# First transfers in order on one queue, the flag through a transfer within SBUF, and spare matmuls in pieces of 176 columns

## The chip, the cores and the metric

One core of a Trainium2 chip. The metric is device time in microseconds of one execution; a median of several executions is given with its range. A profile is one of these executions, and its span is 1.5 to 1.9 us shorter than the device time.

## The reference

```python
# x, f_logit: (4, 6080, 256) fp32; lower_bound: (256,); w_in: (256, 2048), w_out: (2048, 256) float64
f = lower_bound + (1 - lower_bound) * sigmoid(f_logit)
for t in range(S):                          # gated recurrence along the sequence
    h = f[:, t] * h + (1 - f[:, t]) * x[:, t]
    y[:, t] = h
z = y.reshape(24320, 256) @ w_in
out = (z - tanh(z)) @ w_out
```

## The kernel before

The kernel works on blocks of 512 tokens (the first has 256). Weights are 64-bit in memory and are rounded to fp32 on DVE and ACT; block 0 and block 1 are transposed on PE; the recurrence is a scan on DVE; the rest is fp32 matmuls in a Strassen scheme. z - tanh(z) is a polynomial that holds for small z only, so a flag is computed, and at the end every engine reads it and branches over a general version of the kernel. The parts that the change touches:

```python
def fetch_half(u, s, raw, queues):          # first weights: two halves of 256 KB on two queues
    ...
    for i, queue in enumerate(queues):
        part = slice(i * n, (i + 1) * n)
        queue.dma_start(out=dst[:, part], in_=src[s, u][:, part])

def keep_busy(n):                           # spare matmuls on zeros, "K1.n" in the order below
    for _ in range(2 * n):
        nc.tensor.matmul(busy[:, 0:HB], lhsT=zeros..., rhs=zeros...[:, 0:HB], ...)   # HB = 256

def sum_up():                               # the flag: sum over partitions by a matmul
    most = ps_b.tile([P, 2, HB], FP32, name="most", tag="D")
    nc.tensor.matmul(most[0:1, 0, 0:1], lhsT=worst[:], rhs=ones[:], start=True, stop=True)
    nc.scalar.copy(out=flag[:], in_=most[0:1, 0, 0:1])

open_by(["W.0"])                            # first weights, halves on SP and ACT
nc.gpsimd.dma_start(out=lb[:], in_=lower_bound...)
load(0, 0, nc.scalar)                       # f_logit of block 0 on ACT's queue; all else on SP

before = """
    K1.8 ce.0 cr.0 dx.0 cm.0 cx.0 tf.0 cs.0 W.1 tx.0 cb.0 sg0.0 L K1.8 sg1.0 cw.0
    df.1 f0.0 v0.0 f1.0 ce.1 cr.1 v1.0 dx.1 cm.1 cx.1 tf.1 sc0.0 cs.1 W.2 tx.1
    sg0.1 cb.1 sg1.1 sc1.0 K1.1 cw.1 f1.1 F.0.0.0 v1.1 f0.1 W.3 v0.1 cr.2 F.0.0.1
    sc1.1 t.0.0.0 sc0.1 q.0.0.0 K1.3 t.0.0.1 cm.2 F.1.0.0 ...
"""  # issue order: K1 spare, ce..cw weight rounding, tf/tx transposes, sc scans, F matmuls
```

So PE's order is: 16 spare matmuls, transposes of f_logit and x of block 0, 16 spare ones (the second group), transposes of f_logit and x of block 1, 2 spare ones, the first real matmuls (block 0), 6 spare ones (the third group), real matmuls of block 1, and then real work to the end.

Of the kernel before, what the change touches and what calls it, by code (L numbers as in the profile page):

```python
# [9 lines left out]
FP32 = mybir.dt.float32  # L10
# [5 lines left out]
BF16 = mybir.dt.bfloat16  # L16
PSUM = bass.MemoryType.PSUM
P = 128
# [13 lines left out]
def kernel(  # L32
# [25 lines left out]
    nc = tc.nc  # L58

    B, S, D = x.shape  # L60
    DFF = moe_w_in.shape[1]
    N = B * S
    KC = D // P
    TB = 512
    HB = TB // 2
# [18 lines left out]
    const = ctx.enter_context(tc.tile_pool(name="const", bufs=1))  # L84
# [4 lines left out]
    worst = const.tile([P, 1], FP32, name="worst")  # L89
    ones = const.tile([P, 1], FP32, name="ones")  # L90
    flag = const.tile([1, 1], FP32, name="flag")
    zeros = const.tile([P, TB], FP32, name="zeros")
    ident = const.tile([P, P], FP32, name="ident")

# [6 lines left out]
        for s in range(2):  # L101
            queue.dma_start(out=dst[:, :, s], in_=src[s, u])

    def fetch_half(u, s, raw, queues):

        src = moe_w_in.rearrange("(p k) (s u f) -> s u p k f", k=KC, s=2, u=NU)
        dst = raw.rearrange("p (k f) -> p k f", k=KC)
        n = KC // len(queues)
        for i, queue in enumerate(queues):
            part = slice(i * n, (i + 1) * n)  # L110
            queue.dma_start(out=dst[:, part], in_=src[s, u][:, part])

    def fetch_w_out(u, raw, queue):

# [139 lines left out]
    def fast(ctx):  # L254
# [19 lines left out]
        ps_b = ctx.enter_context(tc.tile_pool(name="ps_b", bufs=1, space=PSUM))  # L274
# [9 lines left out]
        order = [(0, 0, 0), (0, 0, 1), (0, 1), (1, 0), (0, 2), (1, 1), (0, 3), (1, 2), (1, 3)]  # L284

        def fetch_weight(i):
            kind, u = order[i][0:2]
            if len(order[i]) == 3:
                raw = Tpool.tile([P, TB], INT64, name="raw", tag="Tg")
                queues = (nc.sync, nc.scalar) if i == 0 else (nc.sync,)  # L290
                fetch_half(u, order[i][2], raw[:], queues)
            else:
                raw = rawpool.tile([P, KC * TB], INT64, name="raw")
                (fetch_w_in, fetch_w_out)[kind](u, raw[:], nc.sync)
            raws[i] = raw
# [256 lines left out]
        def end(j):  # L552


            hb, n = sizes[j] // 2, j * NU + NU - 1
            C = acc[j, "C"][:, 0 : 4 * hb].rearrange("p (n t) -> p n t", n=4)
            osb = opool.tile([P, NQ, D], FP32, name="osb", tag="osb")
            alone = [ps_a.tile([P, TB], FP32, name="A", tag="A")[:, 0:hb] for _ in range(2)]
            for half, (slot, right, q) in enumerate(((A22, "T", 2), (S4, "h", 2))):
                for c in range(2):  # L560
                    nc.tensor.matmul(
                        alone[half],
                        lhsT=w_out[NU - 1][:, slot, c * P : (c + 1) * P],
                        rhs=piece(n, right)[:, q, c],
                        start=c == 0,
                        stop=c == 1,
                    )
            for half in range(2):
                slot = 2 - half
                nc.vector.tensor_tensor(  # L570
                    out=C[:, slot], in0=alone[half], in1=C[:, slot], op=ALU.add
                )
            for half in range(2):
                for i in range(2):
                    name = ("Qa", "Qb", "Qc", "D")[2 * half + i]
                    bank = ps_b.tile([P, KC, P], FP32, name=name, tag=name)
                    for k in (0, 1) if half == 0 else (1, 0):
                        nc.tensor.transpose(
                            bank[:, k], C[:, 2 * k + half, i * P : (i + 1) * P], ident[:]
                        )  # L580
                    (nc.scalar.copy, nc.vector.tensor_copy)[i](
                        out=osb[:, 2 * half + i].rearrange("p (m k) -> p k m", k=KC),
                        in_=bank[:],
                    )
                t0 = starts[j] + half * hb
                nc.sync.dma_start(
                    out=out[t0 : t0 + hb, :].rearrange("(i p) d -> p i d", p=P),
                    in_=osb[:, 2 * half : 2 * half + 2],
                )
# [29 lines left out]
            o3=lambda j: finish(j, 3),  # L619
# [26 lines left out]
        for word in around.split():  # L646
            name, u, at = re.fullmatch(r"([a-zA-Z0-9]+)(?:\.(\d))?([+-]\d)?", word).groups()
# [5 lines left out]
                return natpool.tile([P, NQ, D], FP32, name=name, tag=name)  # L653
            return opool.tile([P, NQ, D], FP32, name=name, tag="osb")

        def load(j, s, queue=nc.sync):

            nat = spot(j, ("fn", "xn")[s])
            queue.dma_start(
                out=nat[:, 0 : sizes[j] // P],  # L660
                in_=srcs[s][starts[j] : starts[j] + sizes[j], :].rearrange(
                    "(n p) d -> p n d", p=P
                ),
            )
            nats[j, s] = nat
# [138 lines left out]
        def p_give(j):  # L804
# [15 lines left out]
            W=fetch_weight,  # L820
            df=lambda j: load(j, 0) if j < TURNED else fetch(j, (0,)),
# [60 lines left out]

        def sum_up():

            most = ps_b.tile([P, 2, HB], FP32, name="most", tag="D")
            nc.tensor.matmul(
                most[0:1, 0, 0:1], lhsT=worst[:], rhs=ones[:], start=True, stop=True
            )
            nc.scalar.copy(out=flag[:], in_=most[0:1, 0, 0:1])

        def turn_and_fetch(j):
            steps["tx"](j)
# [2 lines left out]

        def keep_busy(n):

            for _ in range(2 * n):
                nc.tensor.matmul(  # L899
                    busy[:, 0:HB], lhsT=zeros.bitcast(BF16)[:, 0:P],  # L900
                    rhs=zeros.bitcast(BF16)[:, 0:HB], start=True, stop=True,
                    skip_group_check=True,
                )

# [17 lines left out]
        def open_by(words):  # L922
            for word in words:
                name, *at = word.split(".")
                at = [int(i) for i in at]
                if name in opening:
                    opening[name](*at)
                else:
                    steps[name](at[0] * NU + at[1] if len(at) == 2 else at[0])

        with tc.manual_schedule():
            nc.vector.memset(zeros[:], 0.0)
            nc.vector.memset(ones[:], 1.0)

            open_by(["W.0"])
            nc.gpsimd.dma_start(
                out=lb[:], in_=lower_bound.rearrange("(p k) -> p k", k=KC)
            )
            load(0, 0, nc.scalar)
            make_identity(nc, ident[:])  # L940

            nc.scalar.activation(out=flag[:], in_=ones[0:1, :], func=AF.Sigmoid)
            busy = ps_b.tile([P, TB], FP32, name="B", tag="B")
            open_by(before.split())
            for cycle in range(PLAIN + 1, NBLK + 3):
                for name, u, at in turns:
                    j = cycle + at
                    if not PLAIN <= j < NBLK:
                        continue
                    final = j == NBLK - 1  # L950
                    if final and (name, u) == ("Qd", NU - 1):
                        continue
                    if u is None:
                        if final and name == "o1":
                            nc.vector.reduce_max(
                                out=worst[:], in_=flags[:], axis=mybir.AxisListType.X
                            )
                        if final and name == "o3":
                            sum_up()
                        if final and name == "o4":  # L960
                            end(j)
                        if final and name[0] == "o":
                            if name in ("o1", "o2", "o3"):
                                part_end(j, name)
                            continue
                        steps[name](j)
                        if name == "tx" and j + 1 < NBLK:
                            fetch(j + 1)
                        if final and name == "p15":
                            part_end(j, name)  # L970
                        continue
                    steps[name](j * NU + u)
                    if final and (name, u) == ("Qd", NU - 2):
                        kept = mixpool.tile([P, 4, HB], FP32, name="T")
                        acc[j, "kept"] = kept
                        nc.scalar.copy(
                            out=kept[:, 0:2], in_=acc[j, 3][:, :, 0 : sizes[j] // 2]
                        )
# [172 lines left out]
```

## Time and profile before

| | before |
|---|---|
| time, median of 3 runs | 2329.25 us (2329.11 to 2329.95) |
| span of the profile | 2328.2 us |
| PE busy | 2319.0 us |
| landing of f_logit of block 0 / x of block 1 | 6.73 / 11.50 us |
| last copy ends / last store lands | 2322.78 / 2327.03 us |

PE busy is the whole span (2319.0 of 2328.2 us), so only what moves PE's first real work or what follows its last work can count. The times in the last two rows are from the timeline and from the records of landings. The lines are in the prediction.

The trace's record of a granted clock of 1.00 begins at 10.04 us here. Spare matmuls of 256 columns last 421 ns and start 213 ns apart before it, and last 272 ns and start 109 to 110 apart after it: the prediction and the expectations call this cold or half clock, and warm. In the records of landings f_logit's semaphore rises 16 times, 15 of them by 6.21 us and the last at 6.73, and PE's transposes of it start at 6.86; so the last of the 16 is what I call the landing.

### The profile page before, as it was taken

The numbers are of one execution on the slowest core, as the hardware profiler recorded it, in microseconds if no ns is written. First come the engines' busy times: TensorE is split into PE (matmuls) and PEld (weight loads), VectorE is DVE, ScalarE is ACT, GpSimd is POOL, SyncE is SP. The second block draws the span as 40 slices with busy tenths as digits, with TensorE's granted clock in tenths as the row PEclk, the third lists the DMA queues.
The fourth block names the chain that finished last, engine by engine and source line by source line (L and its number), as shares of the span: only waits on it lengthen the run. The fifth ranks groups of instructions, "written<-read, shape, count | busy, mean of one in ns | idle before, by whom it ended". The sixth has DMA issues, their size and how long they took to land.

```text
span 2328.2 us, 28719 instructions
## 1 busy us (share of the span) xinstructions
PE 2319.0 (100%) x10699; PEld 2027.8 (87%) x10699; DVE 2122.3 (91%) x2451; ACT 1801.8 (77%) x2688; POOL 1.4 (0%) x7
## 2 busy tenths in 40 slices
PE   9999999999999999999999999999999999999998
PEld 6888888888888888888888888888888888888887
DVE  9999899998999989999999999999899998999988
ACT  7777777777777777777777777777777777777775
POOL 0000000000000000000000000000000000000000
PEclk9999999999999999999999999999999999999999
DMA  5301111111111111112111121111211112111101
GB/s 170 70 19 34 39 37 28 28 37 37 37 28 28 39 34 37 28 28 41 32 37 28 28 45 28 37 28 28 46 28 36 28 28 46 31 34 28 28 10 28
DMA packets 296831, 85.00 MB, mean 37 GB/s; under 512 B 289776, under 2 KB 292592, under 8 KB 296688
## 3 DMA queue, kind: packets, MB, share of 16 engines
q1 hardware_dynamic: 296240, 82.61, 16.5%
q8 instruction: 84, 1.38, 0.2%
q14 instruction: 59, 0.48, 0.1%
q10 hardware_dynamic: 416, 0.52, 0.1%
q0 software_dynamic: 32, 0.00, 0.0%
HBM read 58.20 MB, written 24.90 MB: 36 GB/s over the span
## 4 chain that ended last, share of the span: by engine, by line
PE 99%; DMA 0%; DVE 0%; ACTq 0%; issue 0%
PE A L392 27%; PE Qa L475 14%; PE Qb L475 14%; PE D L392 14%; PE Qd L475 14%; PE Qc L475 7%; PE B L392 7%; PE Qa L795 1%; PE Qb L795 1%; PE Qc L795 1%; PE A L728 1%; PE D L728 0%; PE Qd L728 0%; DMA fn<-in_f_logit_dram 0%; PE B L728 0%; PE B L899 0%
## 5 line engine op out<-in xcount | busy, mean ns | idle before, releaser
L392 PE MATMUL A<-T,w_in 128*128 128x256 f32 x2208 | 558.8, 379 | 0.0
L392 PEld LDWEIGHTS A<-T,w_in 128*128 128x128 f32 x2208 | 419.5, 190 | 57.0
L436 DVE TENSOR_TENSOR h<-h,q 128x1024 f32<-128x1024 f32 x368 | 437.4, 1219 | 3.2
L430 DVE SCALAR_TENSOR_TENSOR q<-q,t 128x1024 f32<-128x1024 f32 x368 | 439.8, 1215 | 0.0
L423 ACT ACTIVATE q<-t 128x1024 f32<-128x1024 f32 x368 | 382.7, 1053 | 46.2 <-DVE h L436 43.3
L420 ACT ACTIVATE t<-h 128x1024 f32<-128x1024 f32 x368 | 388.6, 1056 | 3.1 <-DVE h L407 0.3
L441 ACT ACTIVATE junk<-t 128x1024 bf16<-128x1024 f32 x368 | 388.2, 1055 | 1.5
L455 DVE TENSOR_TENSOR Tg<-h 128x1024 f32<-128x1024 f32 x368 | 348.0, 946 | 6.4
L475 PE MATMUL Qb<-h,w_out 128*128 128x256 f32 x1472 | 347.7, 379 | 0.0
L475 PEld LDWEIGHTS Qb<-h,w_out 128*128 128x128 f32 x1472 | 279.7, 190 | 38.0
L475 PE MATMUL Qa<-Tg,w_out 128*128 128x256 f32 x736 | 218.9, 379 | 0.0
L475 PE MATMUL Qa<-h,w_out 128*128 128x256 f32 x736 | 218.9, 379 | 0.0
L404 ACT COPY h<-B 128x512 f32<-128x512 f32 x184 | 107.0, 581 | 144.3 <-PE B L392 95.6
L475 PE MATMUL Qd<-Tg,w_out 128*128 128x256 f32 x732 | 217.7, 379 | 0.0
L475 PE MATMUL Qd<-h,w_out 128*128 128x256 f32 x732 | 217.7, 379 | 0.0
L404 ACT COPY h<-A 128x512 f32<-128x512 f32 x184 | 107.0, 581 | 139.4 <-PE A L392 128.0
L407 DVE TENSOR_TENSOR h<-D,r 128x512 f32<-128x512 f32 x184 | 126.8, 689 | 90.3 <-PE D L392 89.2
L407 DVE TENSOR_TENSOR h<-A,r 128x512 f32<-128x512 f32 x184 | 126.2, 686 | 76.6 <-PE A L392 43.6
L392 PE MATMUL D<-y,w_in 128*128 128x256 f32 x736 | 188.9, 379 | 0.0
L392 PE MATMUL B<-y,w_in 128*128 128x256 f32 x736 | 188.9, 379 | 0.0
L392 PE MATMUL A<-y,w_in 128*128 128x256 f32 x736 | 188.9, 379 | 0.0
L392 PE MATMUL D<-T,w_in 128*128 128x256 f32 x736 | 188.9, 379 | 0.0
(137 smaller groups left out, 2996.6 us busy)
## 6 DMA issues: line engine op xcount, KB each, us to landing
fn<-in_f_logit_dram SPq DMA_DIRECT2D x184, 128.0 KB, 3.1
xn<-in_x_dram SPq DMA_DIRECT2D x184, 128.0 KB, 3.2
out_dram<-osb SPq DMA_DIRECT2D x180, 128.0 KB, 2.8
raw<-in_moe_w_out_dram SPq DMA_DIRECT2D x8, 512.0 KB, 4.5
raw<-in_moe_w_in_dram SPq DMA_DIRECT2D x7, 512.0 KB, 6.6
out_dram<-osb SPq DMA_DIRECT2D x3, 256.0 KB, 4.2
fn<-in_f_logit_dram SPq DMA_DIRECT2D x1, 512.0 KB, 7.4
xn<-in_x_dram SPq DMA_DIRECT2D x1, 512.0 KB, 8.2
```

Source lines behind the costliest of these rows:

```text
L392: nc.tensor.matmul(ps[:, c], lhsT=w_in[u][:, slot, c * P : (c + 1) * P], rhs=mixes[j][right], start=start and c == 0, stop=True, skip_grou ...
L404: nc.scalar.copy(out=dst, in_=piece(n, bank))
L407: nc.vector.tensor_tensor(out=piece(n, "h")[:, q], in0=piece(n, bank), in1=piece(n, r), op=ALU.add)
L420: nc.scalar.activation(out=half(n, i, "t"), in_=half(n, i), func=AF.Square)
L423: nc.scalar.activation(out=half(n, i, "q"), in_=half(n, i, "t"), func=AF.Square, scale=RA, bias=RB,)
L430: nc.vector.scalar_tensor_tensor(out=q, in0=q, scalar=RC, in1=t, op0=ALU.add, op1=ALU.mult)
L436: nc.vector.tensor_tensor(out=h, in0=h, in1=q, op=ALU.mult)
L441: nc.scalar.activation(out=junk[:, :, :, 0 : st[n]["hb"]], in_=t, func=AF.Relu, bias=-TINY, accum_out=flags[:, 2 * n + i : 2 * n + i + 1],)
L455: nc.vector.tensor_tensor(out=o, in0=a, in1=b, op=ALU.subtract)
L475: nc.tensor.matmul(acc[j, part][:, r, 0 : st[n]["hb"]], lhsT=w_out[u][:, slot, c * P : (c + 1) * P], rhs=piece(n, right)[:, q, c], start=( ...
L728: nc.tensor.matmul(h[c], lhsT=w_in[u][:, 2 * k + s, c * P : (c + 1) * P], rhs=ys[j][:, k, 0:nb], start=k == 0 and (c == 0 or len(banks) == 2),
L795: nc.tensor.matmul(acc[j][i // 2][:, i % 2].rearrange("p (k m) -> p k m", k=2), lhsT=plain[j, u][:, s, c, i * P : (i + 1) * P], rhs=w_out[ ...
```

## The change

The intent: let f_logit land sooner by not sharing the queues, take lower_bound off GpSimd's queue (5.5 us from issue to landing there), take the flag's matmul off PE, and cut the spare matmuls finer.

```diff
-            queues = (nc.sync, nc.scalar) if i == 0 else (nc.sync,)
-            fetch_half(u, order[i][2], raw[:], queues)
+            fetch_half(u, order[i][2], raw[:], nc.sync)
...
             for half in range(2):          # end(): the last two additions on DVE
                 ...
+            look()
...
         def sum_up():
-            most = ps_b.tile([P, 2, HB], FP32, name="most", tag="D")
-            nc.tensor.matmul(most[0:1, 0, 0:1], lhsT=worst[:], rhs=ones[:], ...)
-            nc.scalar.copy(out=flag[:], in_=most[0:1, 0, 0:1])
+            nc.sync.dma_start(out=row[:], in_=worst[:])
+        def look():
+            nc.vector.reduce_max(out=flag[:], in_=row[:], axis=mybir.AxisListType.X)
...
-                        if final and name == "o3":     # now right after `worst` is made
                             sum_up()
...
-            for _ in range(2 * n):
-                nc.tensor.matmul(busy[:, 0:HB], ... rhs=zeros...[:, 0:HB], ...)
+            for _ in range(3 * n):
+                nc.tensor.matmul(busy[:, 0:176], ... rhs=zeros...[:, 0:176], ...)
...
-            open_by(["W.0"])
-            nc.gpsimd.dma_start(out=lb[:], in_=lower_bound...)
-            load(0, 0, nc.scalar)
+            nc.scalar.dma_start(out=lb[:], in_=lower_bound...)
+            open_by(["W.0", "df.0"])
```

I call the three parts **queues** (transfers), **flag** and **columns** (spare matmuls).

More of the change, by code (lines that the diff above doesn't have):

```diff
@@ L91 @@
     flag = const.tile([1, 1], FP32, name="flag")
+    row = const.tile([1, P], FP32, name="row")
     zeros = const.tile([P, TB], FP32, name="zeros")
@@ L102, in fetch_w_in, with fetch_half @@
             queue.dma_start(out=dst[:, :, s], in_=src[s, u])
-    def fetch_half(u, s, raw, queues):
+    def fetch_half(u, s, raw, queue):
         src = moe_w_in.rearrange("(p k) (s u f) -> s u p k f", k=KC, s=2, u=NU)
-        dst = raw.rearrange("p (k f) -> p k f", k=KC)
-        n = KC // len(queues)
-        for i, queue in enumerate(queues):
-            part = slice(i * n, (i + 1) * n)
-            queue.dma_start(out=dst[:, part], in_=src[s, u][:, part])
+        queue.dma_start(out=raw.rearrange("p (k f) -> p k f", k=KC), in_=src[s, u])
     def fetch_w_out(u, raw, queue):
@@ L654, in spot, with load @@
             return opool.tile([P, NQ, D], FP32, name=name, tag="osb")
-        def load(j, s, queue=nc.sync):
+        def load(j, s):
             nat = spot(j, ("fn", "xn")[s])
-            queue.dma_start(
+            nc.sync.dma_start(
                 out=nat[:, 0 : sizes[j] // P],
@@ L883, in sum_up @@
         def sum_up():
-            most = ps_b.tile([P, 2, HB], FP32, name="most", tag="D")
-            nc.tensor.matmul(
-                most[0:1, 0, 0:1], lhsT=worst[:], rhs=ones[:], start=True, stop=True
-            )
-            nc.scalar.copy(out=flag[:], in_=most[0:1, 0, 0:1])
+            nc.sync.dma_start(out=row[:], in_=worst[:])
+        def look():
+            nc.vector.reduce_max(out=flag[:], in_=row[:], axis=mybir.AxisListType.X)
         def turn_and_fetch(j):
@@ L896, in keep_busy @@
         def keep_busy(n):
-            for _ in range(2 * n):
+            for _ in range(3 * n):
                 nc.tensor.matmul(
-                    busy[:, 0:HB], lhsT=zeros.bitcast(BF16)[:, 0:P],
-                    rhs=zeros.bitcast(BF16)[:, 0:HB], start=True, stop=True,
+                    busy[:, 0:176], lhsT=zeros.bitcast(BF16)[:, 0:P],
+                    rhs=zeros.bitcast(BF16)[:, 0:176], start=True, stop=True,
                     skip_group_check=True,
@@ L933, in fast @@
             nc.vector.memset(ones[:], 1.0)
-            open_by(["W.0"])
-            nc.gpsimd.dma_start(
+            nc.scalar.dma_start(
                 out=lb[:], in_=lower_bound.rearrange("(p k) -> p k", k=KC)
             )
-            load(0, 0, nc.scalar)
+            open_by(["W.0", "df.0"])
             make_identity(nc, ident[:])
```

## The prediction

> **What bounds the kernel now.** I read the page's summary first, then the waits of the PE alone, then the chain and the timeline of the two ends of the span.
>
> ```profile
> PE 2319.0 (100%) x10699; PEld 2027.8 (87%) x10699; DVE 2122.3 (91%) x2451; ACT 1801.8 (77%) x2688; POOL 1.4 (0%) x7
> ...
> PE 99%; DMA 0%; DVE 0%; ACTq 0%; issue 0%
> ...
> PE B L899 <- DVE ones L933: 1.7, 1, 1.7
> PE Qa L673 <- DMA fn<-in_f_logit_dram: 1.6, 1, 1.6
> ```
>
> The PE is busy for the whole span, the chain that ends last is 99% PE, and the list of PE waits has two entries in the whole run: 1.7 us until the first spare matmul may start, and 1.6 us for the first f_logit block. After that it never stands still until the last stores. So only the first 17 us (before the last gap that is filled with spare matmuls) and the last 10 us can change; the 2300 us between are untouched by the diff. The head, from the chain:
>
> ```profile
> 1.43 5.30 DMA fn<-in_f_logit_dram
> 6.73 0.14 issue
> 6.86 0.67 PE Qa L673 x2
> ...
> 8.82 2.41 PE B L899 x16
> 11.23 0.48 PE Qa L673 x4
> ...
> 13.36 3.46 PE A L728 x16
> 16.82 0.66 PE B L899 x6
> 17.47 1.72 PE Qa L728 x4
> ```
>
> f_logit lands at 6.73 us and from there to 17.47 us the PE is the chain: transposes of block 0, 16 spare matmuls, transposes of block 1, the first real matmuls at 13.36, six spare ones, the next real ones at 17.47. DVE runs nearly full beside it, from the landing of the first weights:
>
> ```profile
> 5.50 0.43 DVE L142 TENSOR_SCALAR e<-raw 128x512 int32<-128x512 int32 x1 [3.85 <-DMA raw<-in_moe_w_in_dram]
> 8.51 0.48 DVE L694 SCALAR_TENSOR_TENSOR v<-fT,om,Qc 128x256 f32<-128x256 f32 x1
> 11.76 0.68 DVE L235 TENSOR_TENSOR_SCAN y<-f,v 128x256 f32<-128x256 f32 x1
> 13.25 0.75 DVE L694 SCALAR_TENSOR_TENSOR v<-fT,om,Qd 128x512 f32<-128x512 f32 x1 [0.23 <-PE Qd L673]
> 14.57 2.45 DVE L235 TENSOR_TENSOR_SCAN y<-f,y,v 128x512 f32<-128x512 f32 x2
> ```
>
> The scan that the first real matmuls need ends at 11.76+0.68 = 12.44, and the one that the matmuls at 17.47 need ends at 14.57+2.45 = 17.02. So the spare matmuls hide little: DVE is at most 0.9 us and then 0.45 us ahead of the PE. That caps what an earlier f_logit can give. The tail, from the timeline:
>
> ```profile
> 2319.14 0.19 PE L886 MATMUL most<-ones,worst 128*1 128x1 f32 x2
> 2321.29 0.42 DVE L570 TENSOR_TENSOR C<-A,C 128x256 f32<-128x256 f32 x1 [0.16 <-PE A L561]
> 2321.77 0.42 DVE L581 COPY osb<-Qb 128x256 f32<-128x256 f32 x1
> 2322.26 0.97 SPq L586 DMA_DIRECT2D out_dram<-osb  x2
> 2322.36 0.42 DVE L581 COPY osb<-D 128x256 f32<-128x256 f32 x1 [0.16 <-PE D L578]
> ```
>
> The flag's matmul sits on PE's path to the end; the last copy ends at 2322.78, and the second of the last stores lands 4.2 us after its issue at about 2322.84, so at 2327.0 of a span of 2328.2.
>
> [...](1) [...]SP and ACT packets alternate from 2.5 us on, and the total is 350 to 390 GB/s with one queue (7 to 14 us) as with two. (2) [...]15 of f_logit's 16 marks are written by 6.24 us, the last at 6.71. (3) [...]The trace records a granted clock of 1.00 only from 10.52 us on, and spare matmuls last 421 ns at first and 272 later. (4) [...]the trace has (3.60-0.42)/15 = 212 ns in the first group and 0.66/6 = 110 ns in the last[...].
>
> **The change part by part.**
>
> *One queue for first weights, f_logit, x.* Before, the two halves of the weights (256 KB each) ran on two queues at once and f_logit queued behind one half while x queued behind the other, so f_logit's packets took turns with x's and with the second weights. In order on one queue the laggard engine writes 16 weight packets of 2 KB, then 16 packets of 1 KB for f_logit (about 45 ns each by the packet records, 0.72 us), then 16 for x. The weights' last mark was at 5.34 us and may come 0.1 us earlier, since no packet of x gets in between; I take 5.2 to 5.3. f_logit's is then 5.25+0.72 = 6.0 instead of 6.71: 0.7 us earlier. x's is 6.7 instead of 6.25, but PE needs it only after four f_logit transposes (0.86 us), so it costs nothing. What follows (second weights, block 1) has the same bytes ahead of it as before and lands as before: the transposes of x of block 1 were due at 3.25+8.2 = 11.45.
>
> *lower_bound on ACT's queue.* It moves 1 KB ahead of everything in place of 7.0 us (issue 1.48 plus 5.5). Its reader ran at 7.85 behind a sigmoid that waited for PE, so it ended no wait. It may put 0.1 us of tiny packets in front of the weights.
>
> *Spare matmuls.* 40 of 256 columns become 60 of 176: 3x176 = 528 columns for 512, 3% more. The first group ends, cold, at 1.71+24x0.147 = 5.2 plus drain, still ahead of f_logit. The second: 24x0.147 = 3.5 us if cold throughout, 24x0.076 = 1.8 if warm (estimates from place 4). Before it took 2.41 with the clock change inside it. The gap in PE's work shrinks from 1.6 to 0.8 us[...]. So: block 0 transposes from 6.1, with x done by 7.9; second group until 9.7 (warm) to 11.0 (cold until 10.5); block 1's last transposes then end by 12.45 (bound by x at 11.45 plus 8 of 0.12) to 12.9; three spare ones 0.23; first real matmuls at 12.7 to 13.1 instead of 13.36.
>
> Next the cap: DVE gains about 0.2 at the start (it waited from cw at 8.39 until Qc for 0.12, and the weights land 0.1 sooner), and its wait of 0.23 for block 1's x shrinks, so its scan ends 0.2 to 0.5 before 17.02. PE's step at 17.47 then comes at about 12.7+3.46+0.68 = 16.85 to 17.2. The head gives **0.3 to 0.65 us, I take 0.55**.
>
> *Flag by a transfer within SBUF.* It removes two matmuls from the PE path (0.12 us in the chain, up to 0.15 with the wait before). It adds a transfer of 128 elements of 4 bytes behind four output stores on SP, issued at about 2319.1; those stores' last marks are at 2321.40, so the row can land at about 2321.6 to 2321.75. The reduce in DVE's stream waits for that, where the last addition now ends at about 2321.6. The reduce takes about 0.25 us (estimate: DVE's copy of 256 columns takes 0.42, half the columns and the same fixed part). So the copy of Qb starts at about 2322.0 for 2321.77; the copy of D, bound by PE until now at 2322.36, stays there; SP's second store is issued about 0.1 later. **Tail: +0.1.** There is one more effect: the flag is known at 2322.0 instead of 2319.5. GpSimd read it at 2319.5 and its instruction fetches ran at 2320.2 and 2322.1, clear of the last stores. Now all engines branch together, and instruction packets meet the stores: in the trace one engine's marks came at 2326.36 and 2327.08, where the other 15 were done at 2325.44, beside an instruction packet of 16 KB that lasted 0.93 us. I add 0.1 for it, with much doubt. Sum: -0.55+0.1+0.1 = about -0.4, so 2329.25-0.4 = **2328.8 us**.
>
> **The rivals.** (a) *DVE becomes the bound in the head*: the weights land no sooner, or later because one queue generates 512 KB in 0.66 us instead of two doing 256 KB in 0.41, and lower_bound's packets precede them. For it: DVE's full timeline from 5.50 to 17 us. Against it: packets started at 2.51, long after both issues. It would leave a gain of 0.1 to 0.2 and a time of 2329.2. (b) *The flag's row lands late*, at 2322.3 or more, and both copies and stores wait: +0.5 to +0.8, time 2329.4 to 2329.7. For it: it queues behind 512 KB of packets of 256 bytes. Against it: those are done by 2321.4. (c) *The laggard engine of the last stores goes free*, because the branches come at another time: up to 2327.08-2325.44 = 1.6 us less, time about 2327.6. (d) *f_logit was hidden anyway* by the spare matmuls: no change in the head, 2329.4. Against it: the recorded 1.6 us wait.
>
> **Range and chances.** The head can give 0 to 0.7, the tail -1.5 to +0.8, and the three runs before spread over 0.84 us: 2327.8 to 2329.8. Two per cent is 46 us, and no end of this kernel has that: 0.99 for within.
>
> **What would show it.** Right: f_logit lands near 6.0, x near 6.7, first real matmuls near 12.8 and the ones after the six (now nine) spare at about 16.9; DVE's wait at 13.25 gone; the reduce ends near 2322.0, D's copy near where it was less the head's gain. Wrong: weights landing after 5.5, a new PE wait on a scan, or a DVE wait of over 0.5 us for the row. A change between 20 and 2310 us would contradict the whole argument.

## The result, and the profile after

| | before | after |
|---|---|---|
| time, median of 6 runs each | 2329.18 us (2328.82 to 2329.95) | 2329.20 us (2329.06 to 2329.84) |
| span of the profile | 2328.2 us | 2327.4 us |

The ratio is 1.0, 95% interval 0.9987 to 1.0013. (The ratio is not quite the ratio of the medians.) The times are the same; the 0.8 us between the two profiles is not a gain, since the profiled run of before (2329.97) was the slowest of its kernel.

The head, in the chain of the kernel after (start, duration, what):

```profile
1.73 4.32 DMA fn<-in_f_logit_dram
...
6.18 0.67 PE Qa L670 x2
...
8.13 2.98 PE B L895 x24
11.11 0.51 PE Qa L670 x4
...
12.10 0.71 PE Qc L670 x4
...
13.52 3.49 PE A L725 x16
17.00 0.68 PE B L895 x9
17.69 1.75 PE Qa L725 x4
```

f_logit lands at 6.04 and PE starts 0.68 us earlier than before (6.18 for 6.86). At 11.11 only 0.12 of that is left, and the real matmuls start later than before: 13.52 for 13.36, 17.69 for 17.47. The list of PE waits agrees with the first half only:

```profile
PE Qa L670 <- DMA fn<-in_f_logit_dram: 0.8, 1, 0.8
```

The recorded wait has halved, from 1.6 to 0.8 us, and the work behind it starts no sooner. On DVE (timeline), the wait for PE's transposes of x of block 1 has grown from 0.23 to 0.38 us, and the scan starts 0.15 later than before:

```profile
13.40 0.75 DVE L691 SCALAR_TENSOR_TENSOR v<-fT,om,Qd 128x512 f32<-128x512 f32 x1 [0.38 <-PE Qd L670]
...
14.72 2.45 DVE L232 TENSOR_TENSOR_SCAN y<-f,y,v 128x512 f32<-128x512 f32 x2
```

The tail (timeline):

```profile
2319.25 0.60 SPq L882 DMA_DIRECT2D row<-worst  x1
...
2321.63 0.27 DVE L885 TENSOR_REDUCE flag<-row 1x1 f32<-1x128 f32 x1
...
2322.02 0.43 DVE L578 COPY osb<-Qb 128x256 f32<-128x256 f32 x1
...
2322.46 0.42 DVE L578 COPY osb<-D 128x256 f32<-128x256 f32 x1
2322.51 0.91 SPq L583 DMA_DIRECT2D out_dram<-osb  x2
```

The row lands 2.3 us after its issue and DVE does not wait for it. The last copy ends at 2322.88, and the last store lands at 2326.34 instead of 2327.03.

### The profile page after: what moved, and what is told of

Read it like the earlier page. It is cut to its first block, busy times and chain, and to the rows that moved or that the text cites. A ratio compares the mean times of both kernels' runs of the same rounds, so it can differ in the third digit from the quotient of the medians.

```text
span 2327.4 us, 28753 instructions
## 1 busy us (share of the span) xinstructions
PE 2319.7 (100%) x10716; PEld 2031.1 (87%) x10717; DVE 2123.0 (91%) x2452; ACT 1801.8 (77%) x2687; POOL 0.7 (0%) x6
## 4 chain that ended last, share of the span: by engine, by line
PE 99%; DMA 0%; DVE 0%; issue 0%; SPq 0%
PE A L388 27%; PE Qa L471 14%; PE Qb L471 14%; PE D L388 14%; PE Qd L471 14%; PE B L388 7%; PE Qc L471 7%; PE Qb L792 1%; PE Qa L792 1%; PE Qc L792 1%; PE A L725 1%; PE D L725 0%; PE Qd L725 0%; PE B L725 0%; DMA fn<-in_f_logit_dram 0%; PE B L895 0%
```

## How I compare profiles: three terms that add up

I ran twelve kernels, so there are 14 profiles. In each I read three times from the timeline: the **landmark** (the first matmul of block 1 after the third spare group: 17.31 before, 17.53 after; the chain gives it 0.16 later), the end of the last copy, and the end of the span. Up to rounding the end is their sum:

| profile | full clock from | x of block 1 lands | landmark | landmark to last copy | last copy to end |
|---|---|---|---|---|---|
| before | 10.04 | 11.50 | 17.31 | 2305.47 | 5.37 |
| after | 10.41 | 11.96 | 17.53 | 2305.36 | 4.52 |
| e1_queue_only | 5.71 | 12.08 | 17.57 | 2305.47 | 5.28 |
| e2_cols_only | 5.46 | 11.44 | 17.01 | 2305.50 | 3.91 |
| e3_flag_only | 5.78 | 11.42 | 16.92 | 2305.33 | 5.36 |
| e4_before_more_spare | 5.57 | 12.07 | 18.66 | 2305.47 | 3.93 |
| f1_before_more_pe_instr | 5.00 | 10.97 | 16.47 | 2305.47 | 3.95 |
| f2_after_256 | 10.63 | 12.08 | 17.58 | 2305.33 | 5.57 |
| f3_after_old_flag | 10.86 | 11.94 | 17.57 | 2305.51 | 3.96 |
| f4_cols_and_flag | 10.13 | 11.05 | 17.59 | 2305.37 | 4.52 |
| g1_split_issue | 7.22 | 11.70 | 17.27 | 2305.50 | 3.90 |
| g2_flogit_first | 10.96 | 12.10 | 17.67 | 2305.51 | 3.89 |
| g3_no_third_group | 11.07 | 11.85 | 17.34 | 2305.58 | 5.03 |
| g4_half_second_group | 10.72 | 11.18 | 16.67 | 2305.51 | 3.96 |

The middle column is the useful surprise: 2305.47 to 2305.58 with the flag's matmul, 2305.33 to 2305.37 without it. So whatever moves the landmark moves the last copy by the same amount, the matmul is worth about 0.14 us, and all other differences sit in the landmark and in the 4 to 5.5 us after the last copy. All timed runs are compared with runs of the kernel before on the same chip. By the record every kernel of this document is "same" as before: the intervals reach about 0.14%, or 3 us, to both sides and include 1 each time. So the differences of medians below are hints, and what carries the argument is the profiles.

## The experiments

### First group: each part alone, and a known delay

**e1_queue_only**: before with the queues part alone.

```diff
-queues = (nc.sync, nc.scalar) if i == 0 else (nc.sync,)
+queues = (nc.sync,)
-open_by(["W.0"]); nc.gpsimd.dma_start(out=lb[:], ...); load(0, 0, nc.scalar)
+nc.scalar.dma_start(out=lb[:], ...); open_by(["W.0", "df.0"])
```

> Kernel before with the queue part of the change alone (first weights, f_logit and x in order on SP, lower_bound on ACT's queue); 256-column spare matmuls and the flag's matmul as before. Landmark: start of the first real matmul of block 1 (after the six spare ones), 17.47 us in the chain of the kernel before and 17.69 after the whole change. My theory: f_logit lands near 6.0, but the second spare group then starts 0.7 us earlier and runs at half clock for that much longer (13 of 16 at 0.213 us), so it ends where it did, and x of block 1 holds the transposes until about 12.0; landmark 17.4 to 17.7, time 2329.2 +- 0.2. Rival 1 (the smaller spare pieces ate the gain): landmark near 17.0, time 2328.7. Rival 2 (the gain of the head is there and the flag's transfer ate it): the same 2328.7.

Measured: 2329.32 us (2328.29 to 2329.86) against 2329.19 of before (nine runs, 2328.07 to 2329.70). Landmark 17.57, so the number is as my theory expected. But its reason was partly wrong: the clock came up at 5.71 us here, so the second group, from 8.47, was over before f_logit of block 1 landed at 10.64, and PE stood waiting for the transfers of block 1. What holds is the other half, x of block 1 at 12.08.

**e2_cols_only**: before with the columns part alone.

```diff
-for _ in range(2 * n):   # 256 columns
+for _ in range(3 * n):   # 176 columns
```

> Kernel before with only the spare matmuls changed from 2n of 256 to 3n of 176 columns. My theory: 3% more columns and nothing else; second group 2.4 to 2.7 us instead of 2.41, landmark 17.5 to 17.7, time 2329.2 to 2329.4. Rival 1 (the pieces cost the gain): second group near 3.0 us, landmark near 18.0, time 2329.7. In both, the clock may rise at another time[...].

Measured: 2328.79 us (2328.26 to 2330.24). Both theories missed: the part that I had thought to cost 0.1 is the one that gains, 0.40 below before by the medians. The landmark is at 17.01, explained by the clock and by x of block 1; what no theory had is the last column, 3.91 us from the last copy to the end instead of 5.37.

**e3_flag_only**: before with the flag part alone (the flag hunks of the diff above).

> Kernel before with only the flag by a transfer within SBUF. My theory: PE is done 0.1 us sooner, the reduce puts 0.25 us into DVE's stream, the last copy of D ends about where it did (within 0.15 us), and the time stays within 0.2 us of before. Rival 2 (the flag's transfer costs what the head gives): the row lands after the last addition, the last copy ends 0.4 us later, time +0.4 or more.

Measured: 2329.43 us (2329.24 to 2329.91), 0.24 above before. Landmark to last copy is 0.14 shorter, as expected, and after the copy it is 5.36, as in before: in the profile the saving reaches the end, but the median does not show it.

**e4_before_more_spare**: a known delay in the head.

```diff
-sc1.1 t.0.0.0 sc0.1 q.0.0.0 K1.3 ...
+sc1.1 t.0.0.0 sc0.1 q.0.0.0 K1.8 ...     # 16 spare matmuls for 6
```

> Kernel before with ten more spare matmuls of 256 columns in the third group, ahead of the first real matmul of block 1: a known delay of 10 x 0.110 = 1.1 us in the head. If PE is the chain from there to the end, as the prediction assumed, the landmark moves to 18.57 and the time by +1.1 us. Rival (slack later in the run swallows what happens in the head): less than +0.5 us.

Measured: 2330.21 us (2329.63 to 2331.02), 1.02 above before. The landmark moved by 1.35 (1.08 of spare matmuls, and x of block 1 landed late) and landmark to last copy stayed 2305.47: the head's time goes through to the last copy one to one. The rival that slack swallows it is out. The time tests this less cleanly, since the 20 PE instructions that this edit adds also changed the last column (3.93).

### What the last column is

The page's list of DMA queues has a kind "instruction":

```profile
q8 instruction: 84, 1.38, 0.2%
```

Each of these 84 packets has 16 KB. The trace of before has 21,467 PE instructions (matmuls, weight loads and the sequencer's own), so there is one packet per 256 (21,467/84 = 255.6), and in the records of packets they follow PE: some 200 to 320 PE instructions lie between one and the next. From these counts I take them for refills of PE's instructions, which is an inference. When the last one comes differs: in before the 84th refill comes at 2324.40, after PE's read of the flag (2321.77), with only 3 PE instructions left; in e2_cols_only, with 40 PE instructions more, it comes at 2313.4. PE's branch itself took 0.36 to 0.37 us in the five profiles with a late refill and 0.22 to 0.23 in the nine others. But PE ran two instructions after the branch (2322.79 and 2323.01) before the packet came, so no run shows it waiting for one. The window of the last stores (2322.6 to 2327.5 us) shows what it falls on. Before:

```profile
q8 instruction: 1, 0.02, 1.2%
q14 instruction: 1, 0.01, 0.4%
...
out_dram<-osb SPq DMA_DIRECT2D x2, 256.0 KB, 4.2
```

After:

```profile
q14 instruction: 2, 0.02, 1.0%
...
out_dram<-osb SPq DMA_DIRECT2D x2, 256.0 KB, 3.0
```

The last number is the time from issue to landing: 4.2 us with PE's refill among the stores, 3.0 without it but with two of the 8 KB packets (q14). In the packet records the two last stores have 32 packets of 4 bytes beside their data, 16 marks each. In before, 15 of the last store's 16 marks are written by 2324.96, and the sixteenth at 2326.60; the store lands at 2327.03. The packet records show why: the refill took 0.93 us from 2324.40, and the packets that were still left of the two stores start at 2325.32, as it ends. That gives a theory: the columns part helps because 40 more PE instructions move the last refill off the last stores, and the flag part hurts because GpSimd, which now learns the flag at 2321.93 instead of 2319.55, branches later (2322.50 for 2320.30) and its 8 KB refill joins them (2323.68 for 2321.63).

### Second group: testing it

**f1_before_more_pe_instr**: no part of the change at all, only more PE instructions where PE waits anyway.

```diff
-K1.8 ce.0 cr.0 ...            # first group: 16 x 256 columns
+K0   ce.0 cr.0 ...            # first group: 36 x 112 columns
```

> Kernel before with its first group of 16 spare matmuls of 256 columns cut into 36 of 112: 40 PE instructions more (20 matmuls, 20 weight loads), all inside the wait for the first f_logit, nothing else changed. New theory: the instruction packets of 16 KB are PE's own refills, one per 256 PE instructions. In the three profiles without added PE instructions the last refill came at 2324.0 to 2324.5 us, after PE's last work and on top of the last stores (last copy to end of span 5.28 to 5.37 us); with 20 or 36 to 40 more it came at 2313.4 to 2318.0, clear of them (3.92, 3.93 and, with the flag's transfer, 4.51 us). So here: last refill near 2313.4, last copy to end 3.9 to 4.0 us, landmark as in the kernel before within 0.1 of 'x of block 1 lands + 5.5 to 5.8', time 1.0 to 1.4 us below before. Rival (the shape of the spare pieces in the second and third group matters, or chance): 5.3 us from copy to end, time as before.

Measured: 2328.07 us (2327.63 to 2329.17) against 2328.98 of before (nine runs, 2327.91 to 2330.08), 0.91 lower. Its last refill came at 2312.9, and the copy-to-end time is 3.95. In its window of the last stores there is no q8 packet:

```profile
q14 instruction: 1, 0.01, 0.4%
```

and the two last stores land in 2.2 and 2.8 us (view of the output tensor, 2320 us to the end):

```profile
DMA to landing us min/median/max: 2.2/2.5/2.8
```

The shape of the later spare pieces is not needed for the gain; 40 more PE instructions are enough.

**f2_after_256**: the changed kernel with the columns part undone.

```diff
-for _ in range(3 * n):   # 176 columns
+for _ in range(2 * n):   # 256 columns
```

> The changed kernel with its spare matmuls put back to 2n of 256 columns (queue part and flag part kept): 40 PE instructions fewer than the changed kernel. New theory: the last refill falls after PE's end again (about 2324), last copy to end of span 5.3 us, time 0.6 to 1.0 us above the changed kernel, so about 2329.9. Rival: tail 4.5 as in the changed kernel and time 2329.2.

Measured: 2330.42 us (2330.17 to 2332.04), 1.44 above before of the same rounds, where the changed kernel was level with before. The refill is back on the stores, with both GpSimd's and PE's packets in the window:

```profile
q8 instruction: 1, 0.02, 2.1%
q14 instruction: 2, 0.02, 1.2%
...
out_dram<-osb SPq DMA_DIRECT2D x2, 256.0 KB, 4.3
```

**f3_after_old_flag**: the changed kernel with the flag's matmul put back (the flag hunks reversed).

> The changed kernel with the flag's matmul put back (queue part and 176 columns kept). New theory: the flag is known at 2319.5 again, GpSimd branches before the last stores, so its 8 KB refill (2323.68 in the changed kernel, during the stores) comes near 2321.3; last copy to end 3.9 us instead of 4.5, PE's end 0.1 later; time 0.3 to 0.6 below the changed kernel, 2328.7. Rival (the prediction's: flag part is worth 0.1): 2329.2, tail 4.5.

Measured: 2328.57 us (2328.43 to 2329.09), 0.41 below before. GpSimd reads the flag at 2319.85, its packet comes at 2321.52, and copy to end is 3.96. In all 14 profiles the 8 KB packet meant here, the second of the tail, follows GpSimd's read of the flag by 1.6 to 2.2 us; that it is GpSimd's refill is inferred from this. Not all of the 0.56 us is the packet's: with the transfer, the last store is issued 0.13 us after the last copy instead of 0.06, and its eighth mark comes 2.44 us after the copy in the changed kernel, for 2.28 here. So some 0.4 is left for the packet.

**f4_cols_and_flag**: before with columns and flag, queues as before.

> Kernel before with 176 columns and the flag's transfer, queues as before. New theory of the head: x of block 1 is what the head waits for, since PE reaches its transposes before it lands whenever the clock comes up early (5.5 us); it lands near 11.4 with two queues and near 12.0 with one, whose first data packet came 0.43 us later (2.46 against 2.03 us). So here x of block 1 lands at 11.4 to 11.5, landmark near 17.0 (17.5 with one queue), last copy to end 4.5, time 0.4 to 0.5 below the changed kernel, 2328.7. Rival (one queue is no worse, only f_logit's landing counts): landmark 17.5, time 2329.2.

Measured: 2329.01 us (2328.53 to 2329.30), level with before (2328.98). Copy to end 4.52, as expected. The landmark missed: x of block 1 landed at 11.05, but the clock came up only at 10.13, f_logit at 6.86, and PE was late at its transposes, as the chain shows:

```profile
8.95 2.46 PE B L900 x24
11.40 0.51 PE Qa L675 x4
...
12.39 0.48 PE Qc L675 x4
```

So the head has two limits, and the later of them counts: x of block 1 (in 9 of the 14 profiles its transposes began 0.13 to 0.14 us after it landed), or PE's own way through the second group, when the clock is late and f_logit too.

How such a wait is read needs care. In e2_cols_only the waits of PE name DVE for it, in f1_before_more_pe_instr the transfer:

```profile
PE Qc L673 <- DVE e L160: 0.3, 1, 0.3
```

```profile
PE Qc L673 <- DMA xn<-in_x_dram: 0.3, 1, 0.3
```

The transposes check semaphores of both (in the trace of after, that of the transfer, last raised at 11.96, and one of DVE). In f1 that DVE step ended at 11.38, after the transposes had begun at 11.11, so DVE is not what they wait for; in e2 it merely ended 0.03 us after the landing (11.47 and 11.44).

### Third group: the queues, and a better head

**g1_split_issue**: f3 with the first weights as two issues of 256 KB on SP.

```diff
-queue.dma_start(out=raw..., in_=src[s, u])
+for part in (slice(0, 1), slice(1, 2)) if s == 0 else ...:
+    queue.dma_start(out=dst[:, part], in_=src[s, u][:, part])
```

> The changed kernel with the flag's matmul put back and the first weights issued as two transfers of 256 KB, still both on SP ahead of f_logit and x. Theory: with one queue the first data packet came at 2.42 to 2.48 us in all four profiles (first issue 0.99 to 1.66 us), with two at 2.01 to 2.03 in all six (0.99 to 1.39), and x of block 1 landed at 11.94 to 12.08 against 10.97 to 11.49 (12.07 once). If the start of the stream waits for the issue of the first transfer, the first packet is back at about 2.02 here, x of block 1 lands near 11.5, landmark 17.0 to 17.2 when the clock comes up near 5.5 us. Rival (one ring is slower whatever the size of its first transfer): first packet at 2.4, x of block 1 at 12.0, landmark 17.55. Last copy to end 3.9 to 4.0 us in both; time 2328.1 to 2328.6.

Measured: 2328.33 us (2327.86 to 2329.21) against 2329.00 of before (nine runs, 2327.92 to 2330.48). First packet at 2.16, x of block 1 at 11.70, landmark 17.27: between the two theories. The size of the first issue may explain a part.

**g2_flogit_first**: before with 176 columns, the first weights on two queues as there, f_logit and x behind them on SP, lower_bound on ACT's queue.

```diff
-open_by(["W.0"]); nc.gpsimd.dma_start(out=lb[:], ...); load(0, 0, nc.scalar)
+open_by(["W.0", "df.0"])       # weights: halves on SP and ACT; f_logit on SP
+nc.scalar.dma_start(out=lb[:], ...)   # after ACT's half
```

> Kernel before with 176 columns; first weights on two queues as before, but f_logit and then x on SP behind one half, and lower_bound on ACT's queue behind the other half. Theory: first packet 2.02, f_logit near 5.8, x of block 1 near 11.4, landmark 16.9 to 17.1 with the clock up early and 17.3 with it late; last copy to end 3.9; time 2328.2 to 2328.7. Rival (f_logit's landing is what counts): landmark near 16.8 whatever the clock, time 2328.0.

Measured: 2328.55 us (2328.03 to 2328.86). The theory missed: the first packet came at 2.01 and x of block 1 still landed at 12.10, landmark 17.67. So the late start of the stream is not the cause. What the slow profiles have in common is that f_logit is on SP with the rest: x of block 1 landed at 11.70 to 12.10 in those seven (mean 11.96) and at 10.97 to 12.07 in the seven with f_logit on ACT's queue (mean 11.37), and by 8 us 1.65 to 1.82 MB had been moved against 1.83 to 1.99. Why more is moved in that stretch with f_logit on ACT's queue is open, and so is whether f_logit's queue is the cause: in all of the first seven, lower_bound is on ACT's queue too, and x of block 1 is issued at 3.78 to 4.23 us instead of 3.25. No run parts the three.

**g3_no_third_group**: g2 without the third spare group (K1.3 removed).

> The kernel of the run before this one without the third group of spare matmuls (nine, 0.68 us), 22 PE instructions more than before. Theory: PE then waits for the second scan of block 1, which ended 0.35 us before the landmark, so the landmark comes at x of block 1 + 5.3 instead of + 5.5 to 5.6: a gain of 0.2 to 0.3; the last refill comes near 2318, last copy to end 3.9; time 2328.0 to 2328.5. Rival (PE is the chain there): a gain of the whole 0.68.

Measured: 2329.54 us (2328.26 to 2329.78), no gain. The landmark is 0.33 earlier than in g2 (17.34), with a PE wait of 0.2 us for the scan in place of the spare matmuls, as the theory had it. But the last refill is back on the stores (2324.2, copy to end 5.03), although 21,489 PE instructions are 22 more than before. The five times fall into 2328.26 and 2328.57, and 2329.54 to 2329.78, as if it went both ways. Eight profiles with 21,491 or more had the early refill, five with 21,462 to 21,467 and 21,489 the late one, and one with 21,486 the early one. So the count alone does not decide it.

**g4_half_second_group**: f1 with the second group cut to half.

```diff
-... sg0.0 L K1.8 sg1.0 cw.0
+... sg0.0 L K1.4 sg1.0 cw.0     # 8 spare matmuls for 16
```

> The kernel with 36 spare matmuls of 112 columns in the first group and the rest as before (the fastest so far, 2328.07), with its second group cut from 16 to 8. Theory: with the clock up early the second group ended 0.2 us before f_logit of block 1 landed and 1.2 us before x of block 1 did, so cutting it changes nothing (landmark = x of block 1 + 5.5); with the clock up late it saves up to 0.5 us. Rival (the group keeps the clock up): PE idle for 1.5 us here, the clock drops or comes later, and transposes and first matmuls last longer (matmuls of 421 ns instead of 283), landmark later by 0.5 or more. Time 2327.8 to 2328.2 or 2328.6 and more.

Measured: 2327.69 us, and the five runs lie within 2327.50 to 2328.03; before had 2329.00 in the same rounds, 2327.92 to 2330.48. The clock came late here (10.72), and PE still began the transposes of x of block 1 only 0.17 us after it landed. The records do show a lower clock after PE stops: in before 0.5 from 2324.28, 1.96 us after PE's last matmul, in after from 2324.64, 2.22 us after it. But one profile does not tell whether the shorter group held the clock back, as the rival had it: in seven other kernels, with the whole group, it came as late (10.04 to 11.07). This is the fastest version, 1.3 us or 0.06% below before. The interval of the ratio, 0.998 to 1.0007, includes 1, so at this size it is likely but not proven.

### The three parts in time

Difference from before of the same rounds, by the medians:

| | 256 columns, matmul flag | 176 columns, matmul flag | 256, transfer flag | 176, transfer flag |
|---|---|---|---|---|
| queues as before | 0 | -0.40 (e2) | +0.24 (e3) | +0.03 (f4) |
| one queue | +0.13 (e1) | -0.41 (f3) | +1.44 (f2) | +0.02 (after) |

Columns gain in all four pairs (0.21 to 1.42), flag costs in all four (0.24 to 1.31), queues cost or do nothing (-0.01 to +1.20). The medians of five to nine runs scatter by some tenths, so the signs are firmer than the sizes; by the intervals no single cell is proven.

## Why the prediction was right or wrong

The time was right (2328.8 against 2329.2, within the range), as was "within 2%". Its steps were not, so that was luck: the range also held "no change", and the errors had opposite signs.

- **Bound: right.** PE's chain carries a head delay through to the last copy (2305.47 in before, e1, e4 and f1).
- **"The head gives 0.3 to 0.65 us, I take 0.55": failed.** In the profile after, the landmark is 0.22 later. f_logit's landing was right (6.04 against 6.0). The step "what follows has the same bytes ahead of it as before and lands as before", with x of block 1 at 11.45, failed: it landed at 11.96, and 0.6 us later on average over seven profiles each. And the second spare group, which I had given 1.8 to 3.5 us, took 2.98 for 2.41 from an earlier start, since the clock came at 10.41 in this run (its pieces of 176 columns started 147 ns apart before that and 76 after it); PE spent on slow spare matmuls what f_logit had given. After that x of block 1 held PE: its transposes began 0.13 us after it landed, where before PE had come to them 0.52 us after. So rival (d), that f_logit was hidden anyway, came nearest. The recorded 1.6 us wait was a wait of an engine whose next wait was 5 us further on.
- **DVE as the cap, rival (a): half right.** DVE's scans moved later, not because of the first weights, which landed 0.17 us sooner (5.31 for 5.48), but behind PE's transposes.
- **Tail to the last copy, +0.1: close in its parts.** The row landed in time (reduce at 2321.63 against my 2321.6 to 2321.75), the reduce took 0.27 against 0.25, and the matmul was worth about 0.14. Rival (b) did not happen.
- **"I add 0.1" for instruction packets: failed in size.** This was the largest effect of all and came in both directions: the flag's late branch costs about 0.6 us after the last copy (4.52 against 3.96 with the matmul put back; some 0.15 of it by the later last store), and the 40 extra PE instructions save about 1.4 where PE's refill had met the stores (5.37 to 3.91; with the flag's transfer 5.36 to 4.52). I had priced the columns part at 3% more columns and never as instructions. Rival (c) is what happened, for a reason that I had not given.
- **Slips.** The packet and clock times that I took from the trace's records were on an axis 0.48 us late: the clock came at 10.04, not 10.52, the first packet at 2.03, not 2.51, and the last marks at 2325.88 and 2326.60. The landings are not touched: f_logit's last mark is at 6.23 and its semaphore rises at 6.73. The terms of the sum give -0.35, which I took as -0.4. And the 350 to 390 GB/s that I read as equal for one queue and two are 338 to 397 from 7 to 14 us and 290 to 382 from 3 to 7.

That nothing came of it in time: the profiles alone would give +0.22 in the head, -0.11 up to the copy and -0.86 after it. But the two profiles are one run each. With f_logit on ACT's queue the landmark varied from 16.47 to 17.59 (e4 less its added 1.08), with it on SP from 17.27 to 17.67. And the long tail cannot be in every run of before: 7 of its 33 timed runs were at 2328.2 or less, spans of 2326.1 to 2326.5, which even with the earliest landmark seen (16.47) leave 4.2 to 4.6 us after the last copy, not 5.4. How often each tail comes in the unprofiled runs is open. What the profiles show is that the parts have effects of opposite sign and of like size: 0.6 us later for x of block 1 with the queues part, 0.5 to 0.6 us more after the last copy with the flag part (0.0 to 0.3 where PE's refill was late anyway), 0.8 to 1.5 us less there with the columns part. That these cancel in the timed runs fits, but is not shown run by run.

## What to carry to other kernels

When one engine is the chain, follow a shortened wait to the next one on that engine before counting it: spare work behind it can stretch (here 2.98 us for 2.41), and a later transfer can be what counts (here x of block 1, landed at 11.96). Count instructions as well as their time: here 40 more on PE, the longest stream, came with its last refill at 2313.4 instead of 2324.40 (e2), off the last stores, and in the changed kernel GpSimd, which learned of its branch at 2321.93 instead of 2319.55, put an 8 KB packet onto them (2323.68). Where a change is worth less than a few microseconds, split the span at fixed landmarks and take several profiles; two runs of the same kernel can differ by more than the change (before had spans of 2326.1 to 2328.7 us).

## What the traces show of the hardware, and what they leave open

- With the 16 KB packet among the last stores, the time from the last copy to the end was 5.0 to 5.6 us (before, e1, e3, f2, g3), without it 3.9 to 4.0, or 4.5 with GpSimd's 8 KB packet there (after, f4). Up to 21,467 PE instructions the last 16 KB packet came late and from 21,491 early, with one of each kind between (21,486 early, 21,489 late). What decides it is open.
- Seven profiles with f_logit on a second queue had x of block 1 landed at 11.37 us on average, seven with it on SP at 11.96, also where the first packet came at the same time (2.01 in g2). I did not find why; lower_bound's queue and the issue time of x changed along with it.
- With the same start of matmuls at 1.70 us, full clock came at 5.0 to 5.8 us in five profiles, at 7.2 in one and at 10.0 to 11.1 in eight. The first stretch of PE's work is 3.6 us long in before, and a wait of 0.6 to 1.6 us follows it in the profiles. No run shows what decides between 5 us and 10.
- A small transfer within SBUF that SP issues, 128 elements of 4 bytes behind 512 KB of stores, landed 2.3 us after issue (after).
